# The opening of a fused attention and gated feed-forward block: five transposed x pieces per block, q/k/v weights in their natural layout, half of them loaded again

## The chip, the cores and the metric

The kernel runs on one core of one Trainium2 chip. The metric is device time in microseconds (us) of one execution. Of the core's engines the text uses these names: PE (matrix multiply; PEld is its weight load), ACT (ScalarE), DVE (VectorE), POOL (GpSimd), SP (SyncE, which issues DMAs here).

## What is computed

x is 2048 tokens by 576, in bf16. It is normalised without scale or bias, goes through windowed causal attention (32 heads of 18, window 256) and through a gated feed-forward part (FFN, 4608 wide), and both results are combined with x:

```python
xn = _layernorm(x)
qkv = (xn @ wqkv).reshape(B, S, 3, 32, 18)
scores = einsum("bhqd,bhkd->bhqk", q, k) * 18 ** -0.5
mask = (i - j >= 0) & (i - j < 256)
s = (softmax(where(mask, scores, -1e9)) @ v) @ wo
h = sigmoid(xn @ w_gate) * (xn @ w_up)
out = x + s * silu(h @ w_down)
```

## The kernel before

The tokens are cut into four chunks of 512 (c = 0 to 3), each into four blocks of 128 (i = 0 to 3). For each chunk the kernel does LayerNorm, the q, k and v projections, attention, the gate and up matmuls of the FFN (36 tiles of 128 columns, in groups of three whose weights go through a ring of buffers), the down projection f2 and the wo projection.

**Half-row matmuls.** 576 is nine pieces of 64. Most matmuls use 64 of the 128 rows of PE; one on the lower and one on the upper half run side by side, and a "pair" below means such two. The lower half walks through the nine pieces of x in the order LO, the upper in the order UP (L32, L33), so xn holds every piece twice: on partitions 0 to 63 in LO's order, on 64 to 127 in UP's. A projection (project, L517) is nine pairs of 288 columns: the lower half makes the first 288 output columns in one PSUM bank, the upper half the other 288 in another. The wqkv buffer follows LO and UP, and is filled by load9 (L403) in four DMAs for each of q, k and v.

**The opening (chunk 0, build_ln, L445).** For each block: an x DMA; two bn_stats (L461, L463) and one bn_aggr (L465) on DVE; rstd by a power on POOL (L468); the normalisation "apply" (L472) and a copy of 64 columns, "wrap" (L476), on DVE; 18 transposes on PE (L498) in two groups; two copies from PSUM to xn on ACT (L510). Ahead of it ten matmuls on a constant tile keep PE at work (warm, L394). In the first two blocks the q projection is cut in two: four pairs that need the first two weight DMAs, then five (L530 to L535). ACT clears the buffers pk (L390) and expr (L391), into which the q and k evacuations (L586) write; v is evacuated at L633.

**Behind the opening.** The gate and up matmuls (L910; ACT takes the tanh, L924, and DVE the product, L928) follow on PE, and the scores of chunk 0 (L697), their exp (L712), masks (L726) and the products with v (L754) are threaded between them. Chunks 1 to 3 get their xn by DMA transposes and use the same wqkv buffer. The weights of f2 (wd) and of wo are loaded during chunk 0, gated on FFN tiles.

**Who sets the order.** Every step is an Op with an engine, a cost in nanoseconds, what it depends on (deps, waits; odeps, order alone) and a priority. schedule (L1158) is a list scheduler: on each engine it takes the enabled op with the least start time plus 40 ns per priority step, and PSUM banks are handed out on the way. What comes out is a fixed order on every engine. emit (L1301) writes it with semaphore waits, so each engine works strictly in that order. Almost all DMAs are issued by SP in one queue.

## Time and profile before

| what | value |
|---|---|
| median of 3 runs | 558.57 us (558.29 to 558.6) |
| the profiled execution | 558.37 us |
| its span on the core | 556.6 us |
| granted PE clock | 1.0 |
| HBM read, written | 55.48 MB, 2.36 MB |

The span is what the profile shows, from the core's first instruction to its last; the profiled execution took 1.77 us more than that. All times of instructions are counted from the start of the span. An instruction's row has its start, its duration, engine, line, operation, and what it writes and reads; brackets behind it hold the idle time of the engine ahead of it and what ended that. Matmuls overlap, so durations of single matmuls don't add up to PE's time; the distance from start to start does.

### The profile page before, as it was taken

How to read it: one execution, taken by the hardware profiler on the slowest of the kernel's cores; microseconds unless marked ns; L12 is line 12 of the kernel's file. 1: busy time of each engine (PE TensorE's matmuls, PEld its weight loads, DVE VectorE, ACT ScalarE, POOL GpSimd, SP SyncE). 2: the span in 40 equal slices, each digit the busy share in tenths (PEclk: the TensorE clock that was granted, in tenths of full speed). 3: DMA queues.
4: the chain of work that ended last, by engine and by line, in shares of the span. 5: the costliest groups of instructions: out<-in, count | busy, mean ns of one | idle time of the engine just before them, and what ended most of it. 6: DMA issues, size and time to landing. Idle time of an engine off the chain costs nothing.

```text
span 556.6 us, 18762 instructions
## 1 busy us (share of the span) xinstructions
PE 551.4 (99%) x8144; PEld 307.7 (55%) x8146; DVE 313.7 (56%) x906; ACT 279.8 (50%) x395; POOL 31.6 (6%) x58
## 2 busy tenths in 40 slices
PE   8999999999999999999999999999999999999998
PEld 5755555567555455556755555545665554554554
DVE  5436998515067988633407798853430785885011
ACT  7436886124076757602408678740330875873031
POOL 3000110100000100010000011001000000000100
PEclk9999999999999999999999999999999999999999
DMA  8999979736956666224994766423369465651001
GB/s 203 221 198 207 215 199 241 203 61 121 210 121 141 142 152 139 60 54 63 137 220 113 152 146 149 104 58 69 73 120 223 103 130 130 145 127 32 21 24 42
DMA packets 125929, 73.35 MB, mean 132 GB/s; under 512 B 54680, under 2 KB 125336, under 8 KB 125848
## 3 DMA queue, kind: packets, MB, share of 16 engines
q1 hardware_dynamic: 125848, 72.16, 60.3%
q8 instruction: 64, 1.05, 0.8%
q14 instruction: 17, 0.14, 0.1%
HBM read 55.48 MB, written 2.36 MB: 104 GB/s over the span
## 4 chain that ended last, share of the span: by engine, by line
PE 98%; DMA 0%; DVE 0%; ACT 0%; issue 0%; SPq 0%
PE ps L910 50%; PE ps L1057 22%; PE ps L524 10%; PE ps L697 6%; PE ps L754 4%; PE ps L824 3%; PE ps L1112 2%; PE ps L1088 2%; DMA xr<-in_A_x_dram 0%; ACT xn L510 0%; PE ps L498 0%; SPq L259 0%; DVE bnst L461 0%; DVE xnr L472 0%; DVE mv L465 0%
## 5 line engine op out<-in xcount | busy, mean ns | idle before, releaser
L910 PE MATMUL ps<-xn,wgs 64*128 64x512 bf16 x2522 | 299.1, 376 | 0.0
L910 PEld LDWEIGHTS ps<-xn,wgs 64*128 64x128 bf16 x2522 | 120.4, 94 | 114.8 <-issue 1.1
L712 ACT ACTIVATE expr<-ps 128x1024 bf16<-128x1024 f32 (+1 forms) x152 | 151.1, 1020 | 25.1 <-PE ps L697 24.8
L928 DVE SCALAR_TENSOR_TENSOR hT<-tring,ps 128x512 bf16<-128x512 bf16 x144 | 98.3, 682 | 53.0 <-PE ps L910 33.5
L924 ACT ACTIVATE tring<-ps 128x512 bf16<-128x512 f32 x144 | 86.5, 601 | 80.9 <-PE ps L910 61.5
L1057 PE MATMUL ps<-wd_sb,hT 64*128 64x512 bf16 (+1 forms) x2016 | 125.5, 283 | 0.0
L1057 PEld LDWEIGHTS ps<-wd_sb,hT 64*128 64x128 bf16 x2016 | 64.6, 94 | 59.7
L726 DVE TENSOR_TENSOR expr<-expr,m 128x256 bf16<-128x256 bf16 (+1 forms) x272 | 60.9, 266 | 8.7 <-ACT expr L712 8.0
L697 PE MATMUL ps<-qkp,kd 64*128 64x320 bf16 (+4 forms) x720 | 56.5, 252 | 0.0
L524 PE MATMUL ps<-wqkv_sb,xn 64*128 64x288 bf16 x864 | 54.4, 283 | 0.3 <-ACT xn L510 0.3
L697 PEld LDWEIGHTS ps<-qkp,kd 64*128 64x128 bf16 x720 | 34.0, 94 | 33.8 <-issue 1.0
L680 DVE TENSOR_SCALAR kd<-qkp,hm 128x256 bf16<-128x256 bf16 x176 | 40.2, 289 | 15.2 <-DMA qkp<-pk 13.2
L1146 ACT ACTIVATE expr<-ps 128x576 bf16<-128x576 f32 (+2 forms) x17 | 9.8, 620 | 77.2 <-PE ps L1057 61.8
L524 PEld LDWEIGHTS ps<-wqkv_sb,xn 64*128 64x128 bf16 x864 | 43.0, 94 | 9.6 <-issue 0.3
L1148 DVE SCALAR_TENSOR_TENSOR expr<-expr,ps 128x576 bf16<-128x576 bf16 x12 | 8.5, 751 | 66.3 <-ACT expr L1146 66.3
L849 ACT ACTIVATE sat<-ps 128x576 bf16<-128x576 f32 x16 | 9.5, 648 | 64.9 <-PE ps L824 64.8
L1150 DVE TENSOR_TENSOR expr<-expr,sat 128x576 bf16<-128x576 bf16 (+2 forms) x17 | 7.2, 436 | 43.6 <-ACT expr L1146 34.4
L770 DVE STREAM_TRANSPOSE pk<-ps 128x512 f32<-128x512 f32 x32 | 21.3, 695 | 17.3 <-PE ps L754 17.3
L736 POOL COPY qkp<-qkp 128x256 bf16<-128x256 bf16 x24 | 12.3, 512 | 261.2 <-DVE kd L680 261.2
L787 DVE STREAM_TRANSPOSE op__63<-pk 128x512 bf16<-128x512 bf16 x32 | 22.3, 702 | 0.1
L754 PEld LDWEIGHTS ps<-expr,vau 64*32 64x32 bf16 x1440 | 18.1, 92 | 7.4 <-issue 6.4
L754 PE MATMUL ps<-expr,vau 64*32 64x320 bf16 (+4 forms) x1440 | 20.8, 254 | 0.0
(55 smaller groups left out, 223.6 us busy)
## 6 DMA issues: line engine op xcount, KB each, us to landing
wgs<-in_B_w_gate_dram SPq DMA_DIRECT2D x47, 240.0 KB, 3.8
wgs<-in_B_w_up_dram SPq DMA_DIRECT2D x47, 240.0 KB, 4.8
wgs<-in_B_w_up_dram SPq DMA_DIRECT2D x47, 192.0 KB, 4.1
wgs<-in_B_w_gate_dram SPq DMA_DIRECT2D x47, 192.0 KB, 4.5
wd_sb<-in_B_w_down_dram SPq DMA_DIRECT2D x9, 576.0 KB, 5.5
xf<-in_A_x_dram SPq DMA_DIRECT2D x18, 144.0 KB, 2.8
out_dram<-xf SPq DMA_DIRECT2D x15, 144.0 KB, 4.4
xr<-in_A_x_dram SPq DMA_DIRECT2D x14, 144.0 KB, 4.2
```

Of the source, the lines that this page charges most:

```text
L524: r = e.matmul(self.bank(ps, HV, hf), self.xn[r0:r0 + 64, k, i * P:(i + 1) * P], self.wqkv_sb[r0:r0 + 64, j, k, :], start=(k == 0), stop=( ...
L680: return e.tensor_scalar(dst, src, self.hm[:, half:half + 1], None, ALU.mult)
L697: i = e.matmul(self.bank(ps, 512, r)[:, pos * 64:(pos + n) * 64], w, self.qkp[r0:r0 + 64, hg, q0 * 64:(q0 + n) * 64], start=True, stop=Tru ...
L712: return e.activation(self.expr[:, es, :, 0:ncol], src, ACTF.Exp, scale=SM_SCALE)
L726: return e.tensor_tensor(ap, ap, m, ALU.mult)
L754: r = e.matmul(self.bank(ps2[s_])[32 * cg:32 * cg + 32, q0 * 64:(q0 + n) * 64], vf[:, v0:v0 + 32], self.expr[p0:p0 + 64, es, cg % 2, pos * ...
L770: tr = self.rd("DVE", dve_ns(CH), lambda e, tf=tf, s_=s_: e.transpose(tf, self.bank(ps2[s_])), f"t1:{c}:{t}", deps=[o, self.op_mul[c][t - ...
L787: t2 = self.op("DVE", dve_ns(CH), lambda e, on=on: e.transpose(self.op_[:, hg % NOT, :], on.rearrange("p g d -> p (g d)")), f"t2:{c}:{hg}" ...
L910: return e.matmul(self.bank((pg, pu)[gu][ft]), w, self.xn[r0:r0 + 64, i, :], start=first, stop=last, tile_position=(r0, 0))
L924: return e.activation(self.tring[:, st_, :], self.bank(ps), ACTF.Tanh, scale=0.5)
L928: return e.scalar_tensor_tensor(self.hT[:, ft, :], self.tring[:, st_, :], 1.0, self.bank(ps), ALU.add, ALU.mult)
L1057: r = e.matmul(self.ps[:, b + n0:b + n1], self.hT[r0:r0 + 64, ft, i * P:(i + 1) * P], self.wd_sb[r0:r0 + 64, q, ft % WDG, n0:n1], start=(s ...
```

## The change

The change rewrites the opening of chunk 0.

- The wqkv buffer gets another layout in the same space: rows of wqkv as they lie in HBM, 128 rows deep and 576 columns wide per 128-row piece; the middle piece (64 rows) lies with its first 288 columns on the lower and its second 288 on the upper half. q, k and v come in by four DMAs each: two of 256 rows by 576 columns, two of 64 by 288. The first q DMA is issued by ACT, behind the memset "pre".
- apply writes 640 columns (0 to 319 and 256 to 575) and wrap is gone in chunk 0. Each block has 10 transposes in place of 18, and one ACT copy of 640 columns in place of two. So xn holds the first five pieces per half in the order LO0/UP0; the other four per half are made by four DVE copies (64 partitions by 4 by 256), which swap lower and upper.
- A projection of chunk 0 (project_swap) runs in three steps: two pairs that need the first weight DMA, three pairs, and four pairs in which lower and upper half swap their output columns. The last step waits until the one before it has ended (a fence).
- The order on PE in the opening is written out by hand (OPEN): w are warm-up matmuls, t the transposes of a block, q0.2 the third step of the q projection of block 0. Warm-up is 8 pairs first, 3 behind t0 and 2 behind q0.0.
- The chunks after the first need the wqkv layout of before. For it half of the buffer is loaded again by 8 DMAs of 64 by 3 by 288 (build_again), behind gate tile 15 of chunk 0 and the last projection of chunk 0.
- The expr buffers are cleared by DVE (one part) and POOL (two), pk still by ACT; small constants change engine or priority. Priorities, slacks and transfer estimates of the x loads change, and bn_aggr gets a priority ahead of other DVE work. In the scheduled program the issue order on SP is: x blocks 0, 1, 2, the three other q DMAs, x block 3, then v and k; DVE does the statistics and aggregate of block 0, those of block 1, then apply of both.

```diff
+LO0 = [0, 2, 4, 5, 7, 1, 3, 6, 8]
+UP0 = [1, 3, 4, 6, 8, 0, 2, 5, 7]
+NC0 = 5
+MID = 4
 HV = D // 2
+WCOL = [0, HV, D, D + HV, 4 * D, 2 * D, 2 * D + HV, 3 * D, 3 * D + HV]
...
-Q_SPLIT = (0, 1)
+LN_STEP = 8
+OPEN = """w0 t0 w1 t1 q0.0 w2 q0.1 q1.0 q1.1 t2 q0.2 q1.2 q2.0 q2.1 v0.0 v0.1 t3 q2.2 v0.2 q3.0 q3.1 v1.0 v1.1 q3.2 v1.2
+v2.0 v2.1 v3.0 v3.1 v2.2 v3.2 k0.0 k0.1 k1.0 k1.1 k0.2 k1.2 k2.0 k2.1 k3.0 k3.1 k2.2 k3.2"""
+OPEN_Y = ("q2", "v0", "v2", "v3", "k2", "k3")
+QKV_AGAIN = 15
+AGAIN_PRIO = 6
+N_FACTOR = 1.2
+AG_PRIO = -20
+XS_ENG = "DVE"
...
-WARM = 10
+WARM = (8, 3, 2)
...
-        self.wqkv_sb = sb("wqkv_sb", [P, 3, NC, HV], bf16)
+        self.wqn = sb("wqkv_sb", [P, 3, NC * HV], bf16)
...
+                self.build_again()
...
-        self.op_negh = op("DVE", 60, lambda e: e.memset(self.neghalf[:, :], -0.5), "neghalf", prio=0)
+        self.op_pre = op("DVE", 450, lambda e: e.memset(self.hT[:, 0, :], 1.0), "pre", prio=-9)
+        ez = [op(eng, 1000, lambda e, k=k: e.memset(self.expf[:, 2 * k:2 * k + 2, :, :], 0.0), f"ez{k}", prio=p)
+              for k, (eng, p) in enumerate((("DVE", -8), ("POOL", 0), ("POOL", 0)))]
+        self.op_ez = ez
+        self.op_negh = op("POOL", 60, lambda e: e.memset(self.neghalf[:, :], -0.5), "neghalf", prio=-5)
...
+        ez[1].odeps.append(self.op_ident)
+        self.op_late = [ez[2], m1]
...
-        self.warm(WARM, "warm:0", [self.op_pre])
-        self.op_pkz = [op("ACT", 1300 + 950, lambda e: e.memzero(self.pk[:, 0:2, :, :]), "pkz", prio=0)]
-        self.op_ez = [op("ACT", 930, lambda e, k=k: e.memzero(self.expr[:, 2 * k:2 * k + 2, :, :]), f"ez{k}", prio=0)
-                      for k in range(QPC - 1)]
-    def warm(self, n, name, deps):
-        ps = Psum((3,))
+        self.op_late += [vo1, h0]
+        for k, n in enumerate(WARM):
+            self.op_open[f"w{k}"] = self.warm(n, f"warm:{k}", [self.op_pre] if k == 0 else [], mm_ns(CH) if k else WARM_NS)
+        self.op_pkz = [op("ACT", 1300 + 1000, lambda e: e.memzero(self.pk[:, 0:2, :, :]), "pkz", prio=-30)]
...
+    def warm(self, n, name, deps, ns):
+        ps = Psum((6, 7))
-                r = e.matmul(self.bank(ps), self.hT[:, 0, 0:P], self.hT[:, 0, :], start=True, stop=True)
+                for hf in range(2):
+                    r0 = 64 * hf
+                    r = e.matmul(self.bank(ps, CH, hf), self.hT[r0:r0 + 64, 0, 0:P], self.hT[r0:r0 + 64, 0, :],
+                                 start=True, stop=True, tile_position=(r0, 0))
-        self.op_warm = self.pe(n * WARM_NS, f, name, deps=deps, prio=-9, psum=[ps])
+        return self.pe(n * ns, f, name, deps=deps, prio=-9, psum=[ps], mode="r64")
...
-        self.op_wqkv = [None] * 3
+        self.op_wqn = [[] for _ in range(3)]
         for j in range(3):
             c0 = j * D
-            self.op_wqkv[j] = self.load9(self.wqkv_sb[0:64, j, :, :], self.wqkv_sb[64:P, j, :, :], wq[:, c0:c0 + HV],
-                                         wq[:, c0 + HV:c0 + D], f"wqkv{j}", ("wqkv", j), [], QKV_LOAD[j], W_FACTOR)
-            for o in self.op_wqkv[j]:
+            nat = self.wqn[:, j, 0:4 * D].rearrange("p (k c) -> p k c", k=4)
+            for k in (0, 2):
+                r0 = k * P + (64 if k else 0)
+                self.op_wqn[j].append(self.dma(
+                    nat[:, k:k + 2, :], wq[r0:r0 + 2 * P, c0:c0 + D].rearrange("(k p) c -> p k c", p=P),
+                    N_FACTOR * 2 * P * D * 2, f"wqn{j}.{k}", ("wqkv", j, k // 2), prio=QKV_LOAD[j], issue=W_ISSUE_NS))
+            for h in range(2):
+                self.op_wqn[j].append(self.dma(
+                    self.wqn[64 * h:64 * h + 64, j, 4 * D:4 * D + HV], wq[MID * 64:MID * 64 + 64, c0 + h * HV:c0 + (h + 1) * HV],
+                    W_FACTOR * D // 2 * P, f"wqn{j}.{4 + h}", ("wqkv", j, 2 + h), prio=QKV_LOAD[j]))
+            for o in self.op_wqn[j]:
                 o.slack = QKV_SLACK
+        o = self.op_wqn[0][0]
+        o.eng, o.prio, o.slack = "ACT", -40, Q_SLACK
+        o.add_dep(self.op_pre)
+        self.op_pkz[0].behind.append(o)
+
+    def build_again(self):
+        again = []
+        for ch in range(NC):
+            if ch != MID:
+                h, c0 = int(WCOL[ch] % D == 0), WCOL[ch]
+                again.append(self.dma(
+                    self.wqn[64 * h:64 * h + 64, :, c0:c0 + HV],
+                    self.wqkv[ch * 64:ch * 64 + 64, :].rearrange("p (j h c) -> p j h c", j=3, h=2)[:, :, h, :],
+                    W_FACTOR * 3 * 64 * D, f"wqa{ch}", ("wqa", ch), deps=self.op_proj + [self.op_f1[(0, QKV_AGAIN)]],
+                    prio=AGAIN_PRIO))
+        self.op_wqkv = [again] * 3
...
-                    f"ag:{st}", deps=[b1, b2, self.op_eps], prio=pr)
+                    f"ag:{st}", deps=[b1, b2, self.op_eps], prio=pr + (AG_PRIO if c == 0 else 0))
...
-            ap = op("DVE", 350, lambda e, st=st, xs=xs, sr=sr: e.tensor_scalar(
-                self.xnr[:, sr, 0:D], xs, self.mv[:, st, 0:1], self.rstd[:, st, :],
-                ALU.subtract, ALU.mult), f"apply:{st}", deps=[rs, ag] + dr, prio=pr)
+            n = DP if c == 0 else D
+            if c == 0:
+                xs = bass.AP(xs.tensor, xs.offset, [xs.ap[0], [D - NC0 * 64, 2], [1, NC0 * 64]])
+            out = self.xnr[:, sr, 0:n]
+            if c == 0:
+                out = out.rearrange("p (g c) -> p g c", g=2)
+            ap = op("DVE", 400 if c == 0 else 350, lambda e, st=st, xs=xs, out=out: e.tensor_scalar(
+                out, xs, self.mv[:, st, 0:1], self.rstd[:, st, :], ALU.subtract, ALU.mult), f"apply:{st}",
+                deps=[rs, ag] + dr, prio=pr)
             ring.release(sx, ap)
-            wr = op("DVE", 100, lambda e, sr=sr: e.tensor_copy(self.xnr[:, sr, D:DP], self.xnr[:, sr, 0:64]),
-                    f"wrap:{st}", deps=[ap], prio=pr)
+            if c > 0:
+                wr = op("DVE", 100, lambda e, sr=sr: e.tensor_copy(self.xnr[:, sr, D:DP], self.xnr[:, sr, 0:64]),
+                        f"wrap:{st}", deps=[ap], prio=pr)
             if st == QPC - 1:
-                self.op_mask[0].odeps.append(wr)
+                self.op_mask[0].odeps.append(ap)
...
-            cols = [k * P for k in range(NKT)] + [64 + k * P for k in range(NC - NKT)]
-            for i0, i1, dep in ((0, XT_CUT, ap), (XT_CUT, NC, wr)):
-                n = i1 - i0
-                ps = Psum((4, 5), (6, 7), (0, 1), (2, 3))
...
+            ps = Psum(*(((4, 5), (6, 7)) if i == QPC - 1 else ((2, 3), (0, 1))))
+
+            def f_tr(e, sr=sr, ps=ps):
+                for k in range(NC0):
+                    for hf in range(2):
+                        r0, b = 64 * hf, ps.banks[hf] * 1024 + 64 * k
+                        r = e.transpose(self.psb[:, b:b + 64], self.xnr[r0:r0 + 64, sr, k * P:(k + 1) * P],
+                                        self.op_[r0:r0 + 64, NOT - 1, r0:r0 + 64])
+                return r
+            tr = self.pe(NC0 * 30, f_tr, f"tr:{st}", deps=[ap, self.op_ident] + dxn, prio=pr, psum=[ps], mode="r64")
...
         if c == 0:
-            for o in self.op_ez[EZ:]:
-                o.odeps += self.op_xn[-1]
+            n = QPC // XS_CUT
+            for a in range(XS_CUT):
+                for hf in range(2):
+                    def f_xs(e, a=a, hf=hf):
+                        cs = slice(a * n * P, (a + 1) * n * P)
+                        src = self.xn[64 * hf:64 * hf + 64, 0:6, cs].rearrange("p (g k) c -> p g k c", g=2)[:, :, 0:2, :]
+                        dst = self.xn[64 - 64 * hf:P - 64 * hf, NC0:NC, cs].rearrange("p (g k) c -> p g k c", g=2)
+                        return e.tensor_copy(dst, src)
+                    self.all_xn.append(op(XS_ENG, XS_NS, f_xs, f"xs:{a}{hf}", prio=3,
+                                          deps=[o for l in self.op_xn[a * n:(a + 1) * n] for o in l]))
...
+                    c0 = WCOL[(LO, UP)[hf][k]]
                     r = e.matmul(self.bank(ps, HV, hf), self.xn[r0:r0 + 64, k, i * P:(i + 1) * P],
-                                 self.wqkv_sb[r0:r0 + 64, j, k, :], start=(k == 0), stop=(k == NC - 1),
+                                 self.wqn[r0:r0 + 64, j, c0:c0 + HV], start=(k == 0), stop=(k == NC - 1),
                                  tile_position=(r0, 0))
...
-        odeps = [after]
-        k0 = 0
-        if c == 0 and i in Q_SPLIT and j == 0:
-            k0 = XT_CUT
-            odeps = [self.pe(k0 * mm_ns(HV), lambda e: f(e, 0, k0), name + ":0",
-                             deps=self.op_xn[i][:1] + self.op_wqkv[j][:2] + deps, prio=1, psum=[ps], mode="r64")]
...
+        if c == 0:
+            return self.project_swap(i, j, name, deps)
+        o = self.pe(NC * mm_ns(HV), lambda e: f(e, 0, NC), name, deps=self.op_xn[i] + self.op_wqkv[j] + deps,
+                    prio=1, psum=[ps], mode="r64", odeps=[after])
...
+    def project_swap(self, i, j, name, deps):
+        ps = Psum(*(((0, 1), (2, 3)) if f"{'qkv'[j]}{i}" in OPEN_Y else ((4, 5), (6, 7))))
+
+        def f(e, steps, swap):
+            for k in steps:
+                for hf in range(2):
+                    r0, n = 64 * hf, hf ^ swap
+                    kx = (0, 1, 3, 4, 2)[k]
+                    c0 = k * D + (n * HV if k < 4 else 0)
+                    r = e.matmul(self.bank(ps, HV, n), self.xn[r0:r0 + 64, kx, i * P:(i + 1) * P],
+                                 self.wqn[r0:r0 + 64, j, c0:c0 + HV], start=(k == 0 and not swap), stop=(k == 3 and swap == 1),
+                                 tile_position=(r0, 0))
+            return r
+        w = self.op_wqn[j]
+        prev = None
+        for n, (steps, swap, d) in enumerate((((0, 1), 0, self.op_xn[i] + w[0:1] + deps), ((2, 3, 4), 0, w[1:]),
+                                              ((0, 1, 2, 3), 1, []))):
+            o = self.pe(len(steps) * mm_ns(HV), lambda e, steps=steps, swap=swap: f(e, steps, swap), f"{name}:{n}",
+                        deps=d, prio=1, psum=[] if prev else [ps], mode="r64", odeps=[prev])
+            if prev:
+                ps.users.append(o)
+            if swap:
+                o.add_dep(prev)
+                o.fence = prev
+            self.op_open[f"{'qkv'[j]}{i}.{n}"] = o
+            prev = o
...
+        if c == 0:
+            order = [self.op_open[w] for w in OPEN.split()]
+            assert len(order) == len(self.op_open)
+            for a, b in zip(order, order[1:]):
+                b.odeps.append(a)
...
-            return e.matmul(self.bank((pg, pu)[gu][ft]), w, self.xn[r0:r0 + 64, i, :], start=first, stop=last,
+            k = i if c > 0 else UP0.index(UP[i]) if half else LO0.index(LO[i])
+            return e.matmul(self.bank((pg, pu)[gu][ft]), w, self.xn[r0:r0 + 64, k, :], start=first, stop=last,
...
```

70 lines of the change are left out of this document (33 added, 37 removed).

## The prediction

> **What bounds the kernel now.** I read the page first: the span, the busy shares, and by line the chain of work that ended last.
>
> ```profile
> span 556.6 us, 18762 instructions
> PE 551.4 (99%) x8144; PEld 307.7 (55%) x8146; DVE 313.7 (56%) x906; ACT 279.8 (50%) x395; POOL 31.6 (6%) x58
> PE ps L910 50%; PE ps L1057 22%; PE ps L524 10%; PE ps L697 6%; PE ps L754 4%; PE ps L824 3%; PE ps L1112 2%; PE ps L1088 2%; DMA xr<-in_A_x_dram 0%; ACT xn L510 0%; PE ps L498 0%; SPq L259 0%; DVE bnst L461 0%; DVE xnr L472 0%; DVE mv L465 0%
> ```
>
> TensorE (PE) is busy 551.4 of 556.6 us and the chain is almost all matmuls. Where are the other 5.2 us? The view of waits, for PE alone, answers: columns are total us, times, longest.
>
> ```profile
> PE ps L399 <- DVE hm L384: 1.5, 1, 1.5
> PE ps L498 <- DVE xnr L472: 0.6, 1, 0.6
> PE ps L524 <- ACT xn L510: 0.3, 1, 0.3
> PE ps L1088 <- issue: 0.2, 1, 0.2
> ```
>
> Three of the four lie in the opening; the rest of the 5.2 us is the tail behind the last matmul. Once the feed-forward matmuls (L910) begin, PE does not stop for anything that this change touches. So the change is worth the shift of the first L910, plus any new stall behind it. The timeline of PE over the first 24 us (start, duration) shows the opening:
>
> ```profile
> 1.52 3.67 PE L399 MATMUL ps<-hT 128*128 128x512 bf16 x10 [1.52 <-DVE hm L384]
> 5.77 1.32 PE L498 MATMUL ps<-op__63,xnr 64*128 64x64 bf16 x36 [0.58 <-DVE xnr L472]
> 7.35 0.67 PE L524 MATMUL ps<-wqkv_sb,xn 64*128 64x288 bf16 x8 [0.25 <-ACT xn L510]
> 7.97 0.54 PE L498 MATMUL ps<-op__63,xnr 64*128 64x64 bf16 x18
> 8.43 1.28 PE L524 MATMUL ps<-wqkv_sb,xn 64*128 64x288 bf16 x18
> 9.55 0.43 PE L498 MATMUL ps<-op__63,xnr 64*128 64x64 bf16 x18
> 9.81 11.82 PE L524 MATMUL ps<-wqkv_sb,xn 64*128 64x288 bf16 x190
> 21.45 2.77 PE L910 MATMUL ps<-xn,wgs 64*128 64x512 bf16 x24
> ```
>
> The first projection starts at 7.35, the first L910 at 21.45: 14.10 us. The last 95 pairs (190) take 9.81 to 21.45, 0.1225 a pair; all 108 pairs are 13.23. Eighteen transposes take 0.26 (9.55 to 9.81), so two sets leave about 0.35 of waiting in the 14.10. The opening is therefore nearly full once it runs, and the gain must come from an earlier 7.35.
>
> **Part 1: when the first projection starts.** What leads there is the LayerNorm of block 0 and, on DVE, of block 1. Rows of the timeline, then two of the chain in order of time, and the ACT copy out of PSUM by its form:
>
> ```profile
> 3.05 0.46 DVE L461 BATCH_NORM_STATS2 bnst<-xr 128x6 f32<-128x288 bf16 x1 [1.08 <-DMA xr<-in_A_x_dram]
> 3.43 0.44 DVE L463 BATCH_NORM_STATS2 bnst<-xr 128x6 f32<-128x288 bf16 x1
> 4.59 0.57 POOL L468 TENSOR_TENSOR rstd<-mv,neghalf 128x1 f32<-128x1 f32 x1 [0.82 <-DVE mv L465]
> 5.10 0.20 DVE L465 BATCH_NORM_AGGREGATE mv<-bnst 128x2 f32<-128x15 f32 x1
> 5.22 0.41 DVE L472 TENSOR_SCALAR xnr<-xr,mv,rstd 128x576 bf16<-128x576 bf16 x1
> 1.26 2.64 DMA xr<-in_A_x_dram
> 6.10 1.20 ACT xn L510 x2
> L510 ACT ACTIVATE xn<-ps 128x640 bf16<-128x640 bf16 x4 | 2.8, 706 | 0.0
> ```
>
> Block 0 lands at 3.05, block 1 at 3.90 (1.26 + 2.64). In the changed order DVE does both statistics and the aggregate of block 0, then those of block 1, then the normalisation of block 0. So block 1's landing X1 sets that normalisation: X1 + 0.03, a pitch of 0.38 (3.05 to 3.43), 0.44, some 0.06 to the aggregate, 0.12 (5.10 to 5.22): X1 + 1.03. The other input, rstd of block 0, would be ready at 4.8 and is no longer last. Is X1 still 3.90? The change puts 295 KB of q weights on ACT's queue behind the first DVE memset (about 1.5), beside the x blocks. DMA engines over short windows (length; busy of PE, PEld, DVE, ACT, POOL; clock, DMA share, GB/s):
>
> ```profile
> 1.75:2.50 0.75, 0.75 (x3) 0.30 (x2) 0.12 (x2) 0.74 (x2) 0.61 (x4) 1.00 0.72 204
> 2.50:3.25 0.75, 0.75 (x4) 0.20 (x3) 0.20 (x1) 0.75 (x2) 0.75 (x2) 1.00 0.93 235
> 4.00:4.75 0.75, 0.75 (x4) 0.35 (x3) 0.75 (x4) 0.75 (x2) 0.16 (x1) 1.00 0.52 124
> 1.75:6.70 4.95, 4.20 (x36) 1.65 (x34) 3.71 (x16) 3.88 (x6) 3.05 (x7) 1.00 0.82 220
> 1.75:10.00 8.25, 7.24 (x112) 3.99 (x112) 6.05 (x24) 6.86 (x11) 4.15 (x9) 1.00 0.91 232
> ```
>
> By 2.5 us 153 KB have moved; of the 295 KB of blocks 0 and 1, 142 are left, 0.6 us at 235 GB/s. If ACT's transfer shares the engines from 2.7 on, the last 95 KB take 0.8 instead of 0.4. So X1 lies between 3.9 and 4.3; I take 4.2, nearer the shared end since the engines are already 0.93 busy. [...]
>
> With 4.2 the normalisation starts at 5.23. It is 640 wide instead of 576: 0.41 becomes 0.46. Transposes start 0.14 after its end as before (5.63 to 5.77): 5.83. The copy began 0.33 after the first transpose (5.77 to 6.10); two more transposes add 0.03: 6.19. One copy of 640 takes 0.71 and PE follows in 0.05: the first projection at **6.95**, 0.40 earlier. The second block's transposes and the 3 warm-up pairs between fit inside this time (normalisation of block 1 ends near 6.5).
>
> **Part 2: from there to the first L910.** All 108 pairs stay: 13.23. Two warm-up pairs now stand inside; a 512-wide pair costs 1.94 / 9 = 0.216 by the pace of the FFN tiles:
>
> ```profile
> 43.09 0.60 ACT L924 ACTIVATE tring<-ps 128x512 bf16<-128x512 f32 x1 [1.34 <-PE ps L910]
> 45.03 0.60 ACT L924 ACTIVATE tring<-ps 128x512 bf16<-128x512 f32 x1 [1.34 <-PE ps L910]
> 53.41 0.60 ACT L924 ACTIVATE tring<-ps 128x512 bf16<-128x512 f32 x1
> 74.04 0.60 ACT L924 ACTIVATE tring<-ps 128x512 bf16<-128x512 f32 x1
> ```
>
> That is 0.43. The transposes of blocks 2 and 3 are 10 each: 2 x 0.145 = 0.29 by the 0.26 for 18. One wait is new: block 2's transposes stand behind two projections' first passes, 6.95 + 0.43 + 10 pairs (1.23) = 8.61. Its normalisation waits for rstd of block 1 (aggregate 5.11 to 5.31, POOL 0.57, so 6.0), then normalisation 1, two statistics, aggregate, rstd and normalisation 2 by the same steps: 8.73, transposes at 8.87. Wait 0.26. Behind it the whole projection queue of PE waits. Block 3 follows about 2.2 us later, when PE still has 18 pairs: no wait. The fences (a swapped pass waits until the first pass of the same projection has ended) cost nothing, since other passes (0.6 us or more) stand between. Sum: 6.95 + 13.23 + 0.43 + 0.29 + 0.26 = **21.16**, against 21.45: a gain of 0.29 us.
>
> The weights must come in time. The second q piece is needed at 7.6, the last v piece at 10.85. Ahead of them lie 1.1 MB and 1.92 MB; by the two long windows above 1.09 MB had moved by 6.70 and 1.91 MB by 10.0, and a landing shows 0.6 to 0.8 us behind its last byte: 7.4 and 10.7. That is just in time; the half-empty stretch at 4.0 to 4.75 (0.52) would be filled by ACT's transfer, 0.1 MB or 0.4 us more. I cost lateness at nothing, with 0.5 us each as the other end.
>
> **Part 3: what lies beside.** Two memsets of expr, 128x1024, move from ACT to DVE and POOL, and a third to POOL behind the four rstd. On DVE one costs twice the 485 ns of the row below, from 1.46 to 2.43, before block 0 lands at 3.05; POOL has until 4.2 for its first, and ACT has only the q issue (0.62) before it in place of them. SP keeps 11 of the 12 weight issues, so the FFN weights behind them come no later. The planner also moves some score units of chunk 0 by a few L910: same work, PE fed either way, cost nothing, up to 0.5 us if an exp comes late. The four copies of x pieces are 64x1024 bf16 on DVE. Nearest rows:
>
> ```profile
> L372 DVE MEMSET hT<- 128x512 bf16 x1 | 0.5, 485 | 1.0 <-PEq L1408 1.0
> L382 DVE COPY m<-m 64x192 bf16<-64x192 bf16 x1 | 0.2, 203 | 0.0
> L633 DVE CAST vau<-ps 64x288 bf16<-64x288 f32 x8 | 3.7, 457 | 1.7 <-PE ps L524 1.5
> L399 PE MATMUL ps<-hT x10: 379/620/634, 1.5 to 4.8; 128*128 128x512 bf16 x10
> ```
>
> Grown by elements, the SBUF copy gives 1.1 us a piece, the PSUM cast 1.6; ungrown, 0.2. I take 0.6, between the copy's ends, since part of its 0.203 does not grow. All four are needed only by the first L910, and PSUM banks are handed back over 2 us before reuse, so 2.4 us in all hide there and 6.4 would delay an evacuation or two (up to 0.5 us).
>
> The reload: 8 DMAs of 110 KB behind tile 15 (53.41; one tanh of L924 a tile, counted from 0), 0.885 MB, on SP ahead of the weight group for tiles 24 to 26.
>
> ```profile
> 54.70 0.62 SPq L259 DMA_DIRECT2D wgs<-in_B_w_up_dram  x1
> 60.23 0.59 SPq L259 DMA_DIRECT2D wgs<-in_B_w_gate_dram  x1
> wgs<-in_B_w_gate_dram SPq DMA_DIRECT2D x1, 240.0 KB, 3.7
> 55.00:75.00 20.00, 20.00 (x346) 11.05 (x342) 19.11 (x65) 16.76 (x22) 3.51 (x5) 1.00 0.94 229
> ```
>
> SP is free from 55.3 to 60.23; 8 issues at 0.62 and one x load behind a DVE wait end near 61.3, so the group starts 1 us late. Its four DMAs, issued until 63.8, landed after some 4 us, 67.9; the reload's bytes at 229 GB/s put 3.9 us ahead of them. 72.8 against the need at 74.0 (tile 23's tanh): hidden, with 1.2 us to spare. The weights are read again only in chunk 1, over 40 us later.
>
> **Rivals.** *Loads late*: x block 1, the second q piece or the last v piece come up to 0.5 us each after PE wants them. For: the margins above are 0.1 to 0.2, the DMA share 0.9. Against: SP's dip is filled. Two of three late by 0.45 give +0.9: **559.0** (no gain left, +0.6 on before).
> *Reload not hidden* (slower): decides from 6.1 us (67.9 to 74.0) of delay. At half the DMA rate, as 124 GB/s in one window above, the bytes take 7.1, with 1.0 of issue 8.1: PE stands 2.0 us at tile 24, **560.1**. Against: 229 GB/s over twenty us there.
> *Slow clock* (slower): the ten warm-up matmuls shorten from 0.63 to 0.38 and take 3.28 us from first to last start; with a pitch of 0.216 when fast and twice that when slow, six are slow: the clock rises some 2.7 us after 1.52. The changed warm-up ends near 4.8, and PE then pauses 1.0 us, not 0.58. If the clock falls back and needs those 2.7 us again, work from 5.83 to about 9 runs at half speed: 1.5 to 1.9 us lost, **559.8**. Against: 0.58 did no harm. [...]
> *No shortcut* (the earlier start is eaten): X1 at 4.6 makes the start 7.35 and the end 21.56, **558.5**; part of "same".
> *Much faster* would need the first L910 before 20.3; even with X1 = 3.9 and no wait it is 20.6 (**557.5**).
>
> **How the numbers follow.** The profiled execution took 558.37 us, 1.77 around its span; the median of the runs is 558.57, 0.2 above. Forecast: 558.37 - 0.29 = **558.1**. Chances: forecast (557.5 to 558.5, no-shortcut included) 0.54; loads late 0.26; reload 0.07; clock 0.07; something faster than I can derive 0.06. About 0.2% (1.1 us) is what a measurement tells from no change. Forecast and late loads both lie within it: same 0.80; slower 0.14; faster 0.06. The range reaches from the best sum to past the late loads: 557.5 to 559.3.
>
> **What would show it.** Right: first transposes near 5.8, first projection near 6.95, first L910 near 21.2, a short wait at block 2's transposes, no PE wait between 22 and 118. Wrong: a PE wait on a wqkv DMA; a wait before an L910 near 74; a projection pitch above 0.1225 before 10 us; block 1's statistics after 4.3.

## The result, and the profile after

The changed kernel takes **560.07 us** (median of 8 runs, 560.04 to 560.44) against 558.57 (558.14 to 558.60); the ratio is 1.003, 95% interval 1.0019 to 1.0041. The prediction said 558.1, range 557.5 to 559.3: it missed by 2.0 us and on the wrong side. The profiled execution took 560.04, its span is 558.3; the lines below answer to those of before, first the page, then the waits of PE.

```profile
span 558.3 us, 18736 instructions
...
PE 552.4 (99%) x8128; PEld 312.9 (56%) x8130; DVE 318.9 (57%) x906; ACT 274.9 (49%) x388; POOL 32.1 (6%) x61
```

```profile
PE ps L552 <- DVE xnr L526: 1.6, 2, 1.1
PE ps L422 <- DVE hT L385: 1.5, 1, 1.5
```

PE still bounds the kernel, but a wait of 1.1 us for a normalisation (L526 is the changed apply) has come in. PE's timeline shows which (L422 warm-up, L552 transposes, L608 projections, L1004 feed-forward):

```profile
1.52 3.60 PE L422 MATMUL ps<-hT 64*128 64x512 bf16 x16 [1.52 <-DVE hT L385]
5.55 0.45 PE L552 MATMUL ps<-op__63,xnr 64*128 64x64 bf16 x10 [0.44 <-DVE xnr L526]
5.79 1.41 PE L422 MATMUL ps<-hT 64*128 64x512 bf16 x6
7.02 0.32 PE L552 MATMUL ps<-op__63,xnr 64*128 64x64 bf16 x10
7.17 0.42 PE L608 MATMUL ps<-wqkv_sb,xn 64*128 64x288 bf16 x4
...
8.82 0.32 PE L552 MATMUL ps<-op__63,xnr 64*128 64x64 bf16 x10
8.97 2.38 PE L608 MATMUL ps<-wqkv_sb,xn 64*128 64x288 bf16 x36
12.48 0.32 PE L552 MATMUL ps<-op__63,xnr 64*128 64x64 bf16 x10 [1.12 <-DVE xnr L526]
12.62 10.06 PE L608 MATMUL ps<-wqkv_sb,xn 64*128 64x288 bf16 x160
22.50 3.85 PE L1004 MATMUL ps<-xn,wgs 64*128 64x512 bf16 x34
```

Block 2's transposes (8.82) start without a wait; those of block 3 stand from 11.36 to 12.48, and the first L1004 comes at 22.50 where 21.16 was forecast and 21.45 stood before. What DVE did then, and POOL beside it:

```profile
8.12 0.45 DVE L526 TENSOR_SCALAR xnr<-xf,mv,rstd 128x640 bf16<-128x640 bf16 x1 [0.76 <-PE ps L422]
...
10.29 2.04 DVE L526 TENSOR_SCALAR xnr<-xf,mv,rstd 128x640 bf16<-128x640 bf16 x1
```

```profile
9.63 0.55 POOL L516 TENSOR_TENSOR rstd<-mv,neghalf 128x1 f32<-128x1 f32 x1 [1.65 <-DVE mv L513]
10.13 0.95 POOL L386 MEMSET expr<- 128x1024 f32 x1
11.02 0.26 POOL L397 MEMSET m<- 128x192 bf16 x1
11.21 0.94 POOL L408 MEMSET vau<- 128x192 bf16 x1
12.21 0.35 POOL L409 MEMSET vau<- 128x228 bf16 x1
```

The same operation takes 0.45 for block 2 and 2.04 for block 3, and it ends 0.18 us behind POOL's third memset in a row (11.21 + 0.94 = 12.15; 10.29 + 2.04 = 12.33). The fourth starts at 12.21, 0.06 behind the third's end, and the normalisation is over 0.12 later, 0.23 ahead of the fourth's own end.

Comparing starts on PE, the changed kernel is later by 1.05 at the first L1004, by 1.34 from the eighth feed-forward tile on, by 1.59 at chunk 1's first projection, by 1.70 from the last chunk's down-projection on. So three smaller losses follow the large one: 0.29, 0.25 (0.24 by the rows below) and 0.11. The second is this pair of rows, before and then after:

```profile
120.09 2.24 PE L1057 MATMUL ps<-wd_sb,hT 64*128 64x512 bf16 x40
122.17 4.08 PE L524 MATMUL ps<-wqkv_sb,xn 64*128 64x288 bf16 x64
```

```profile
121.44 2.24 PE L1152 MATMUL ps<-wd_sb,hT 64*128 64x512 bf16 x40
123.76 2.50 PE L588 MATMUL ps<-wqkv_sb,xn 64*128 64x288 bf16 x38
```

From the last down-projection group to the projection pass 2.08 us before, 2.32 after. In the program the first projection of chunk 1 now waits for 11 semaphores; 8 of them are those of the reload.

### The profile page after: what moved, and what is told of

The parts are those of the page before. It is cut to its first block, busy times and chain, and to the rows that moved or that the text cites. A ratio compares the mean times of both kernels' runs of the same rounds, so it can differ in the third digit from the quotient of the medians.

```text
span 558.3 us, 18736 instructions
## 1 busy us (share of the span) xinstructions
PE 552.4 (99%) x8128; PEld 312.9 (56%) x8130; DVE 318.9 (57%) x906; ACT 274.9 (49%) x388; POOL 32.1 (6%) x61
## 3 DMA queue, kind: packets, MB, share of 16 engines
q8 instruction: 64, 1.05, 0.8%
## 4 chain that ended last, share of the span: by engine, by line
PE 98%; DVE 1%; DMA 0%; issue 0%; ACT 0%; DVEq 0%
PE ps L1004 50%; PE ps L1152 22%; PE ps L588 7%; PE ps L790 6%; PE ps L847 4%; PE ps L917 3%; PE ps L608 2%; PE ps L1207 2%; PE ps L1183 2%; DVE xnr L526 0%; DMA xr<-in_A_x_dram 0%; PE ps L422 0%; PE ps L552 0%; DVE bnst L509 0%; DVE bnst L511 0%
## 5 line engine op out<-in xcount | busy, mean ns | idle before, releaser
L1004 PE MATMUL ps<-xn,wgs 64*128 64x512 bf16 x2522 | 299.7, 376 | 0.1
L1004 PEld LDWEIGHTS ps<-xn,wgs 64*128 64x128 bf16 x2522 | 122.4, 94 | 112.8 <-issue 1.4
L1152 PEld LDWEIGHTS ps<-wd_sb,hT 64*128 64x128 bf16 x2016 | 65.8, 94 | 58.5
L790 PE MATMUL ps<-qkp,kd 64*128 64x320 bf16 (+3 forms) x720 | 56.9, 252 | 0.0
L588 PE MATMUL ps<-wqkv_sb,xn 64*128 64x288 bf16 x648 | 40.7, 283 | 0.1
L588 PEld LDWEIGHTS ps<-wqkv_sb,xn 64*128 64x128 bf16 x648 | 33.0, 94 | 6.5 <-issue 0.2
L829 POOL COPY qkp<-qkp 128x256 bf16<-128x256 bf16 x24 | 10.9, 456 | 255.5 <-DVE kd L773 255.5
```

The lines of the kernel that those rows point to most:

```text
L588: r = e.matmul(self.bank(ps, HV, hf), self.xn[r0:r0 + 64, k, i * P:(i + 1) * P], self.wqn[r0:r0 + 64, j, c0:c0 + HV], start=(k == 0), stop ...
L790: i = e.matmul(self.bank(ps, 512, r)[:, pos * 64:(pos + n) * 64], w, self.qkp[r0:r0 + 64, hg, q0 * 64:(q0 + n) * 64], start=True, stop=Tru ...
L1004: return e.matmul(self.bank((pg, pu)[gu][ft]), w, self.xn[r0:r0 + 64, k, :], start=first, stop=last, tile_position=(r0, 0))
L1152: r = e.matmul(self.ps[:, b + n0:b + n1], self.hT[r0:r0 + 64, ft, i * P:(i + 1) * P], self.wd_sb[r0:r0 + 64, q, ft % WDG, n0:n1], start=(s ...
```

## The experiments

Theories at the start: **A**, POOL's memsets keep DVE out while block 3's normalisation runs (1.1 us); **B**, the split warm-up raises PE's rate later than full-row matmuls do; **C**, the reload's semaphores cost PE 0.24; **D**, a DVE product of the feed-forward part is late because of its place in the program (0.29). Two more come up on the way: **B2**, too little warm-up lets PE's full rate come late in some executions; **E**, the reload makes weight groups late near 76 us. Times are medians, with the ratio to the kernel before and its 95% interval.

### POOL's memsets and block 3

```diff
-                    o.odeps.append(rs)
+                    o.add_dep(ap)
```

> The changed kernel, with one edit: POOL's late work (two memsets of 128 columns and more, one of expr 128x1024, the mask) is ordered behind the normalisation of block 3 (L526) instead of behind its rstd (L516). Theory A (the 2.04 us normalisation of block 3, beside POOL's memsets at 10.13 to 12.56, is DVE being kept out by POOL): that normalisation takes 0.45 again, block 3's transposes start where PE reaches them, about 11.4, without the 1.12 us wait; the first feed-forward matmul comes at 21.4 instead of 22.50; time 560.07 - 1.1 = 559.0. Rival (the normalisation is long for a reason of its own: it stands behind a PSUM cast and reads two overlapping pieces): it stays near 2 us, 560.1. Second rival (the gain is eaten because the late memsets now collide with DVE's PSUM casts and the x copies that follow): normalisation 0.45, but casts of 1 us or more behind it and 559.5 or above.

**558.94 us**, 1.0012 (1.0003 to 1.0022): 1.1 less than the changed kernel. DVE's row, then PE's:

```profile
10.29 0.45 DVE L526 TENSOR_SCALAR xnr<-xf,mv,rstd 128x640 bf16<-128x640 bf16 x1
```

```profile
11.34 0.32 PE L552 MATMUL ps<-op__63,xnr 64*128 64x64 bf16 x10
...
21.36 2.99 PE L1004 MATMUL ps<-xn,wgs 64*128 64x512 bf16 x26
```

The same start, 0.45 instead of 2.04, and no wait of PE for block 3. Theory A holds; the second rival is there in small, since DVE's copies of x pieces now meet the memsets (two of them 1.37 instead of 0.88), and the first L1004 still comes 1.1 us earlier than in the changed kernel.

The other direction, the suspected cost added to the kernel before:

```diff
+            if st == QPC - 1:
+                self.op_extra = [op("POOL", 1000, lambda e, k=k: e.memset(
+                    self.hT.bitcast(dt.float32)[:, 1 + 4 * k:5 + 4 * k, :], 0.0), f"extra{k}", prio=-30) for k in range(2)]
```

> The kernel before, with two added memsets of 128x1024 (f32 words) on POOL right behind the rstd of block 3 (L468), onto hidden-layer columns that the first tiles overwrite later: 1.9 us of POOL work that nothing waits for. Theory A (POOL's memset keeps DVE out of SBUF): the normalisation of block 3, 0.43 in the kernel before, starts near 8.72 and ends only with the memsets near 10.5 to 10.7; block 3's transposes move from 9.55 to 10.7 or 10.9, and the time grows by 1.2 to 1.3 us to 559.8. If only the memset that is running keeps it out and the next one lets it in: end near 9.9, +0.3 to +0.5, 559.0. Rival (the two engines do not meet; the length came from elsewhere): normalisation 0.43, time unchanged at 558.57.

**559.43 us**, 1.0020 (1.0010 to 1.0029), 1.0 more than the kernel before in the same series (558.43). POOL, DVE, PE:

```profile
8.43 1.84 POOL L472 MEMSET hT<- 128x1024 f32 x2
```

```profile
8.62 1.81 DVE L477 TENSOR_SCALAR xnr<-xf,mv,rstd 128x576 bf16<-128x576 bf16 x1 [0.68 <-POOL rstd L468]
```

```profile
1.52 4.45 PE L399 MATMUL ps<-hT 128*128 128x512 bf16 x10 [1.52 <-DVE hm L384]
...
10.58 0.46 PE L503 MATMUL ps<-op__63,xnr 64*128 64x64 bf16 x18 [0.63 <-ACT pk L591]
```

In the kernel before, POOL has nothing behind its last rstd, and the normalisation follows it:

```profile
8.03 0.55 POOL L468 TENSOR_TENSOR rstd<-mv,neghalf 128x1 f32<-128x1 f32 x1 [0.78 <-DVE xnr L476]
```

```profile
8.72 0.43 DVE L472 TENSOR_SCALAR xnr<-xf,mv,rstd 128x576 bf16<-128x576 bf16 x1 [0.68 <-POOL rstd L468]
```

In the run with the added memsets 0.43 has become 1.81: the operation lasts until both memsets are over (10.27; it ends at 10.43), not until the one that was running is. The bracket of the last PE row names an ACT copy (L591), but in the kernel before the same transposes start at 9.55, ahead of that copy (9.82), so they do not need it; 0.15 behind the normalisation's end fits. A is shown from both sides, and two more profiles with the changed kernel's opening (one semaphore, and the reload behind tile 24, both below) have the wait of PE too, 1.33 and 1.24.

### The semaphores of the reload

```diff
-                    W_FACTOR * 3 * 64 * D, f"wqa{ch}", ("wqa", ch), deps=self.op_proj + [self.op_f1[(0, QKV_AGAIN)]],
+                    W_FACTOR * 3 * 64 * D, f"wqa{ch}", ("wqa",), deps=self.op_proj + [self.op_f1[(0, QKV_AGAIN)]],
```

> The changed kernel, its eight reload transfers counted on one semaphore instead of one semaphore each: the first projection of chunk 1 on PE then waits for 4 semaphores, not 11. Theory C (the 0.24 us that PE loses between the last down-projection and that projection, 2.32 against 2.08, is paid for reading seven more semaphores, 0.03 us each): the gap is 2.08 to 2.12 again and the time 559.8. Rival (the reload or the block's transposed input lands late): the gap stays 2.32 and the time 560.07.

```profile
121.37 2.24 PE L1152 MATMUL ps<-wd_sb,hT 64*128 64x512 bf16 x40
123.45 2.74 PE L588 MATMUL ps<-wqkv_sb,xn 64*128 64x288 bf16 x42
```

The gap is 2.08 again: theory C holds in the profile (0.24 for seven waits, 0.034 each). Other profiles agree: 2.31 to 2.35 in three more with eight semaphores, 2.07 to 2.08 in six more with one. The times do not show it: 559.73, 559.85, 560.47, 560.59, 560.85 (median 560.47, 1.0036, 1.0023 to 1.0050); only the 559.73 was profiled, and what made the three upper ones is open. Both repairs together:

> Both repairs that are not in dispute: POOL's late work behind the normalisation of block 3 (1.1 us), and one semaphore for the reload (0.24 us). If they add: 560.07 - 1.13 - 0.24 = 558.7. If one of them only uncovers another wait: 558.9.

**559.1 us**, 1.0019 (1.0009 to 1.0028); ten times from 558.62 to 560.57, the profiled one 558.66. In it PE's gap ahead of chunk 1 adds nothing, so the two add up; but the times spread over 2 us, which neither the changed kernel nor the one before does, and why is open: the profiled execution is one of the fast ones.

### The late product

```diff
+        for k in range(8):
+            pads.append(op("DVE", 70, lambda e: e.memset(self.hm[:, :], 0.0), f"pad{k}", deps=pads[-1:], prio=4))
```

> As the run with POOL's late work behind the normalisation of block 3, and eight more memsets of 128x2 on DVE, one behind the other, ahead of the one that was there: they only move DVE's instructions from there on by eight places. Theory D (the hidden-layer product of tile 5 is 0.43 us late because of its place in DVE's stream of instructions, where the next piece of the program is fetched): the delay leaves tile 5 and falls eight instructions earlier or elsewhere, PE's extra 0.28 to 0.30 us at tile 7 goes, and the time is 558.94 - 0.3 = 558.65. Rival (the delay belongs to that time, from the transposing transfers then under way): the same product is late by the same amount, time 558.94.

**558.71 us**, 1.0011 (1.0001 to 1.0020). The products of the run without the eight memsets (tiles 4 and 5), then of the run with them (tile 1):

```profile
32.05 0.69 DVE L1022 SCALAR_TENSOR_TENSOR hT<-tring,ps 128x512 bf16<-128x512 bf16 x1 [1.25 <-ACT tring L1018]
34.42 0.69 DVE L1022 SCALAR_TENSOR_TENSOR hT<-tring,ps 128x512 bf16<-128x512 bf16 x1 [1.68 <-PE ps L1004]
```

```profile
26.45 0.69 DVE L1025 SCALAR_TENSOR_TENSOR hT<-tring,ps 128x512 bf16<-128x512 bf16 x1 [1.68 <-PE ps L1007]
```

The idle time ahead is 1.68 instead of 1.25 (0.43 late); PE, which needs that PSUM bank two tiles on, loses 0.3. Eight instructions moved it by four products; a product waits for two semaphores, so two places for each would fit, but that count is argued. So the delay is not bound to a time, it moves with what stands ahead in DVE's stream: theory D, as far as that. It did not go away: PE lost 0.24 by the tenth tile all the same. The 0.11 late in the program is absent here.

The other profiles add to this. Seven of them have the vau memsets of POOL behind rstd 3 or behind block 3, and no added memsets on DVE: in all seven tile 5's product is late by 0.42 to 0.44, and tile 9's of the last chunk by 0.36, from which the 0.11 comes. The seven with these two memsets moved to POOL's start (further below) show neither, although in six of them the trace counts the same 44 DVE instructions ahead of the first product; so does the kernel before, and no product is late there. So the number of counted instructions alone does not decide (waits are not counted). That the fetching of the program is the cause was only argued, and stays open.

### The warm-up

```diff
+                if full:
+                    r = e.matmul(self.bank(ps, CH, k % 2), self.hT[:, 0, 0:P], self.hT[:, 0, :], start=True, stop=True)
```

> As the run with POOL's late work behind the normalisation of block 3, and the first eight warm-up pairs (two matmuls of 64 rows each, side by side) written as eight matmuls of 128 rows, as the kernel before has them. Theory B (the two-half pairs do not raise the clock as full-row matmuls do): the pitch falls from 0.43 to 0.22 at about 4.2, all of the second group of three pairs and block 0's transposes run fast, the first projection starts at 6.7 to 6.95 instead of 7.34, and the time is 0.3 to 0.4 us below that run, 558.6. Rival (the clock rises at a fixed time or by how long PE has been busy, whatever the form): the pitch still halves only near 7, the first projection at 7.3, same time as that run, 559.0.

559.32 us, 1.0018 (1.0008 to 1.0027); first projection at 7.34. There is no gain, ten times from 558.80 to 560.45 against 558.81 to 559.62 without the edit: this does not bear theory B out. The reverse:

> The kernel before, with its ten warm-up matmuls of 128 rows written as ten pairs of 64-row halves, nothing else. Theory B (half-row pairs do not raise the clock in time): the pitch stays at 0.43 throughout, the warm-up ends at 5.8 instead of 5.2, block 0's transposes and the first projections run at half pace until about 7.5; the first projection starts 0.3 to 0.5 us later than 7.35 and the time is 0.4 to 1.0 us higher, 559.0 to 559.5. Rival (the form does not matter): pitch halves near 4.2, 558.57 as before.

558.84 us, 1.0006 (0.9997 to 1.0016), first projection at 7.42, the warm-up 4.45 us long: 0.4 above the kernel before, with an interval that takes in 1, so inconclusive. The row at 1.52 of the run with added POOL memsets, above, says why: there the unchanged ten full-row matmuls took 4.45 us, all at the slow pitch of 0.43, where the profile of before has 3.67. **When PE's full rate comes differs from execution to execution of the same warm-up.** The runs with the spread reload, without the reload and with the reload behind tile 24 (all below) begin with the same ten half-row pairs, and these took 3.73, 4.33 and 4.45 us; why is not shown. The granted clock reads 1.00 in all these stretches (1.75 to 2.50 in the kernel before, where the pitch is slow), so it does not show the change; that the clock makes the pitch fall from 0.43 to 0.22 was argued and is not shown. Does it matter how much work the warm-up keeps up?

> As the run with both repairs, and one pair of warm-up matmuls instead of three between block 0's transposes and block 1's. Theory B (these pairs run at 0.40 to 0.43 a pair while PE is still slow, so they hold back block 1's transposes, which could start 0.14 us behind their normalisation's end at 6.38): block 1's transposes at 6.5 instead of 7.05, first projection at 6.85 instead of 7.33, and 0.3 us of it is left at the first feed-forward matmul, since block 2's normalisation (end 8.57) is next late: 558.4. Rival (PE then idles longer, and the full rate comes later or a q weight transfer is late): first projection earlier, but its matmuls at half pace, no gain at the first feed-forward matmul, 558.7 or above.

559.13 us, 1.0015 (1.0006 to 1.0024), times from 558.60 to 560.06. The profiled execution is the 560.04:

```profile
6.86 0.66 PE L608 MATMUL ps<-wqkv_sb,xn 64*128 64x288 bf16 x4
7.29 1.08 PE L422 MATMUL ps<-hT 64*128 64x512 bf16 x4
8.15 2.15 PE L608 MATMUL ps<-wqkv_sb,xn 64*128 64x288 bf16 x16
```

Eight pairs from 8.15 to 10.07, 0.24 a pair, twice the later pace. In this execution the rival came true: the first projection is early, but the full rate comes only near 10, and the first L1004 at 22.76. That the two pairs left out are the reason is not shown: with all three the times spread as far (558.62 to 560.57, above). And in the kernel before:

```diff
-WARM = 10
+WARM = 8
```

> The kernel before, with eight warm-up matmuls instead of ten, nothing else. Theory B2 (the pause ahead of block 0's transposes makes the full rate come late in some executions): some of the ten times go up by 0.5 to 1.5 us, median 558.8 or above, highest near 559.8, against 558.1 to 558.6 for the kernel before. Rival (two matmuls do not matter): 558.1 to 558.6 as before.

559.15 us, 1.0009 (1.0000 to 1.0019): four times at 558.20 to 558.35, six at 559.07 to 559.54; the kernel before in the same series, 35 times, 558.17 to 558.63. So two warm-up matmuls fewer cost about 1 us in some executions. The profiled one was of the lower group, so that the clock is the reason is argued, not shown.

### What is late next

The profile with both repairs has a new wait, ACT and PEld:

```profile
14.04 0.84 ACT L726 ACTIVATE vau<-ps 64x288 bf16<-64x288 f32 x2 [1.65 <-POOL vau L409]
```

```profile
15.32 5.90 PEld L608 LDWEIGHTS ps<-wqkv_sb,xn 64*128 64x128 bf16 x98 [0.40 <-ACT expr L679]
```

Put behind block 3, the vau memsets are late for the copies of v. POOL has room for them: in the changed kernel it is idle from 2.34 to 4.26.

```diff
-        vo1 = op("POOL", 1100, lambda e: e.memset(self.vau[:, :, :, 0:H // 2, DH:DH + 1], 1.0), "vones", prio=1)
+        vo1 = op("POOL", 1100, lambda e: e.memset(self.vau[:, :, :, 0:H // 2, DH:DH + 1], 1.0), "vones", prio=-3)
...
-        self.op_late += [vo1, h0]
+        self.op_late += [h0]
```

> As the run with both repairs (POOL's late work behind block 3's normalisation, one semaphore for the reload), and the two memsets of vau (0.94 and 0.3 us) put on POOL ahead of the expr memset, into its idle time between 2.3 and 4.26. In that run POOL's memsets ended at 13.96, two copies of v out of PSUM waited for them, and PE lost 0.4 us near 15. Theory: the copies start at 13, PE's loss near 15 goes, the first feed-forward matmul comes at 21.05 instead of 21.35, time 558.66 - 0.3 = 558.35 in the executions with an early clock. Rival (the PSUM banks come back late for another reason, DVE's copies of x pieces at 0.69 each beside the expr memset): PE's wait near 15 stays, time 558.65.

POOL now has them from 1.40 to 2.68. The lowest of ten times is 557.98, the median 559.0 (1.0012, 1.0001 to 1.0022), the highest 561.04. The first L1004 is at 20.96, 0.49 ahead of the kernel before, and no wait is left near 15: right. But half the times lie above 559.5; the profiled one (559.54) loses 1.3 us at 76, not in the opening. With ten warm-up pairs (`WARM = (10, 3, 2)`):

> As the run with the early vau memsets, and ten warm-up pairs ahead of block 0's transposes instead of eight. Theory B2 (the time at which PE's full rate comes differs from execution to execution; eight pairs end at 5.1 and leave 0.4 us idle before block 0's transposes, so the full rate can come as late as 10; ten pairs at 0.43 fill the time to 5.8): the slow executions at 559.5 to 560.6 go, and the spread of ten times shrinks from 2 us to 0.6 us, the median falls to 558.4 or below. Rival (the spread has nothing to do with the warm-up): spread as before, from 558.3 to 560.5.

**558.25 us**, 0.9998 (0.9990 to 1.0006), eleven times from 557.87 to 558.79 and one at 560.41, which is the one profiled:

```profile
77.37 1.45 PE L1004 MATMUL ps<-xn,wgs 64*128 64x512 bf16 x11 [1.61 <-issue]
```

A feed-forward matmul is late by 1.61. High times are rarer (1 of 12 against 5 of 10), but the two that were profiled, one in each run, lost their time at 76 and not to a late full rate, so theory B2 is not shown by them. With sixteen tiny DVE memsets besides:

> As the run with ten warm-up pairs, and sixteen tiny memsets on DVE (128x2 bf16 each, onto a hidden-layer tile that is overwritten), six in its idle time near 7.5 and ten near 16 to 20. Theory D (a product of the hidden layer is 0.44 us late because of its place in DVE's stream; eight more instructions moved the delay from tile 5 to tile 1): with sixteen it falls ahead of tile 0, among the copies out of PSUM, and PE does not lose 0.3 us in the first tiles, nor 0.1 us late in the program; time 0.3 to 0.4 us below the run without them, 558.0. Rival (some product is late in any case): no difference to that run.

558.39 us, 0.9999 (0.9991 to 1.0008): no difference. No product was late in the run without them either, so the memsets had no delay to move.

### The reload

The wait near 76 falls where the weight groups issued behind the reload are used. Leaving the reload out:

> As the run with ten warm-up pairs, without the reload: the weights of q, k and v stay in their first layout, so chunks 1 to 3 multiply with weights of other rows (that part of the computation is changed). It prices the reload's bytes and issues by leaving them out. Theory E: no wait at 76, all times between 557.85 and 558.4. Rival (the waits come from elsewhere): spread as with the reload, 557.9 to 560.4.

558.09 us, 0.9994 (0.9986 to 1.0003), all eleven times within 557.86 to 558.63; this kernel leaves out the right weights for chunks 1 to 3, so it is a price and no version to use. Spreading it:

```diff
-                    W_FACTOR * 3 * 64 * D, f"wqa{ch}", ("wqa",), deps=self.op_proj + [self.op_f1[(0, QKV_AGAIN)]],
+                    W_FACTOR * 3 * 64 * D, f"wqa{ch}", ("wqa",), deps=self.op_proj + [
+                        self.op_f1[(0, (7, 9, 11, 12, 0, 14, 15, 17, 18)[ch])]],
```

> As the run with ten warm-up pairs, early vau memsets and both repairs; the eight transfers of the reload, which stood together behind tile 15, are gated by tiles 7, 9, 11, 12, 14, 15, 17 and 18, so that one to three of them stand between weight groups. Theory E (PE's waits of 1.3 to 1.6 us at 76 are weight groups late behind 0.885 MB in one lump): the same bytes leave earlier, no wait at 76, nothing later in SP's queue moves, times 557.85 to 558.5 with none at 559 or above. Rival (the DMA engines have no room for these bytes anywhere between 40 and 76): waits there as before or earlier, highest times 560 and above.

558.38 us, 1.0003 (0.9994 to 1.0012); nine times within 557.89 to 558.66, two at 559.84 and 559.89. Neither better nor worse than the lump. Moving it back (`QKV_AGAIN = 24`):

> As the run with ten warm-up pairs, early vau memsets and both repairs, and the reload of the q, k and v weights gated by tile 24 of the feed-forward part instead of tile 15, so that it stands behind the weight groups of the tiles that are needed next and in the stretch from 75 to 85, where the kernel before left the DMA engines 0.56 to 0.69 busy. Theory E (the 1.3 to 1.6 us that PE waited at 76 in two profiled executions is a weight group that the reload had delayed): no PE wait near 76, and the times that were above 558.6 (up to 560.4) go; all between 557.85 and 558.5, median 558.0. Rival (those waits are not from the reload): spread as before, 557.9 to 560.4.

562.28 us, 1.0065 (1.0052 to 1.0079). The wait at 76 is gone, but the reload stands ahead of wd and of the next chunk's transposes in SP's queue, and PE waits 1.1 us for wd and 0.9 for a transposed oT. With eight warm-up pairs:

> The same with eight warm-up pairs, as the changed kernel has them. Theory B2 (the pause before block 0's transposes makes the full rate come late in some executions, as in the kernel before with eight): some times are 0.5 to 1.5 us higher than with ten, in two groups. Rival (the spread in the changed kernel's family came from the reload alone): same times as with ten pairs, 557.85 to 558.5.

561.96 us, 1.0057 (1.0044 to 1.0069): these waits hide what the warm-up does, so this one is inconclusive. And in the changed kernel alone:

> The changed kernel with the reload gated by tile 24 instead of tile 15 and nothing else. Theory (in the changed kernel itself the reload was hidden, its feed-forward part started 1 us later): 560.05 as before, spread 0.4. Rival (part of its 1.5 us came from the reload): below 559.8.

564.13 us, 1.0098 (1.0084 to 1.0111), 4 us worse, which neither side expected. Its waits of PE:

```profile
PE ps L1152 <- DMA wd_sb<-in_B_w_down_dram: 2.7, 2, 1.5
...
PE ps L917 <- DMA oT<-op__63: 0.9, 1, 0.9
```

Behind tile 15 the reload cost the changed kernel nothing; behind tile 24 it costs 4 us. Where the feed-forward part starts 1.3 to 1.5 us earlier than in the changed kernel (at 21.16 and 20.96 instead of 22.50), PE waits 1.6 and 1.3 us in the profiled executions even behind tile 15. With the reload there, 1 of 12, 5 of 10 (eight pairs), 2 of 11 (sixteen memsets) and 2 of 11 (spread) times lie above 558.8, without it none of 11. With ten pairs that is 5 of 34 against none of 11, which by itself could be chance. The landings say more. The weight group issued from 66.6 or 66.8, the second behind the reload, took 8.8 to 9.7 us to land in both stalled executions; its second and third transfers landed near 76.5 and 77.5, on either side of 77.30 and 77.37, where PE went on. The same group took 5.6 to 7.6 in the profile with sixteen memsets, which does not stall, and 3.8 to 5.3 without the reload. So late weights fit the wait, and in these profiles they land later with the reload ahead of them. Why only some executions come to a wait stays open, and so does whether the earlier start is the reason, since the reload and the weight groups are gated by tiles and move with it.

## Why the prediction was wrong, point by point

**The step that failed** stands in part 2 and part 3: "Block 3 follows about 2.2 us later, when PE still has 18 pairs: no wait", with the memset that goes "to POOL behind the four rstd" given no price. Timing of data and queue were right: block 3's normalisation started 2.17 behind block 2's, rstd 3 ended at 10.18, and without POOL's work the normalisation would have ended at 10.74 (10.29 + 0.45) and the transposes could have started 0.14 later, before PE came at 11.36. Instead the normalisation lasted until 12.33 and PE waited 1.12. Only one of the three memsets in its way is in the prediction: those of m and vau (0.26 and 0.94), at 1.15 and 2.49 in the kernel before, were moved behind rstd 3 as well (op_late in the diff) and are not in the sum. What was not asked is how long the normalisation takes beside POOL's memsets. The rows of before could not show it, since there POOL was idle from 8.58 on. The traces show it held through two memsets in a row (1.81 us instead of 0.43) and through three (2.04 instead of 0.45); how the memsets hold it is not shown. As an estimate from the rows, a hold by the first memset alone would have ended the normalisation near 11.53 (11.08 + 0.45), and PE would have waited 0.3 us, not 1.12.

**The opening before that** was about right. Block 1 landed by 4.09 (4.2 taken), the normalisation of block 0 started at 5.02 (5.23), its transposes at 5.55 (5.83). The first projection came at 7.17 instead of 6.95: the copy out of PSUM was over at 6.74, but the three warm-up pairs between, said to fit inside this time, ran at 0.41 a pair from 5.79 to 7.02. In six other profiles with eight pairs and this order the first projection came at 6.80 to 6.95, in one at 7.33. The late rate cost the changed kernel nothing, since block 3's wait takes it up. The wait of 0.26 at block 2 was not there.

**The sum.** Forecast for the first L1004: 21.16; measured 22.50. Of the 1.34, 1.12 is block 3's wait, the rest some 0.15 of late arrival there and 0.07 on the last 80 pairs.

**Three terms that were missing**: the semaphores of the reload (0.24, shown by one semaphore in their place), the late product at tile 5 (0.29, moved by eight instructions, cause open), and 0.11 in the last chunk, which comes with a second late product. Against the kernel before, 1.05 + 0.29 + 0.24 + 0.11 = 1.69, against 1.7 between the spans.

**What lies beside** held in part: the copies of x pieces took 0.44 (0.6 taken), and no q, k or v weight was late. The reload was hidden in the changed kernel, but in the run with ten warm-up pairs the feed-forward part starts at 21.16, just as forecast, and PE waits 1.61 at 76 in the profiled execution. Part 3 followed only the first weight group behind the reload: 72.8 was forecast, and in that execution it landed by about 72.1. The group behind it, issued from 66.8, took 8.8 to 9.7 us to land, where the kernel before shows 4.2 to 4.7 for the group at that place.

**The rivals.** None named the cause. "Slow clock" gave 559.8 and "Reload not hidden" 560.1, both close to 560.07 and for other reasons: the full rate did come late, but to the cost of nothing here, that a pause of PE brings the slow rate back is not shown, and PE has no wait near 74.

**Is there a better version?** With late memsets, early vau memsets, one semaphore and ten warm-up pairs the median is 558.25, ratio 0.9998 (0.9990 to 1.0006): no measurable difference to the kernel before. At the first feed-forward matmul the profiles of such versions gain 0.3 to 0.5 us (0.29 was forecast; the run with sixteen memsets loses 0.1 instead), and the reload takes it back now and then. Even without the reload the gain in time, 0.45 between the medians, has an interval that takes in no change.

## What to carry to other kernels

When work is moved to an engine that is idle, ask what its neighbours do at that moment, not only whether its own engine is free: beside 2.0 us of POOL memsets a DVE operation of 0.45 us took 2.04, on the path. A transfer that is hidden has a margin: whatever makes its consumers earlier, or it later, spends that margin (the reload behind tile 24 instead of tile 15 took the changed kernel from 560.07 to 564.13). And an edit on the warm-up must be judged over many executions, since one profile shows one of several times at which PE's full rate comes (the same ten matmuls took 3.67 and 4.45 us).
